# Token scores made by 32 rows in four column quarters and turned back, one weight product for all batches, and small operations moved to GpSimd

## The chip, the cores and the metric

One core of one Trainium2 chip runs the whole program. The metric is the time of one execution in device microseconds (us); the figure before is the median of three runs. A separate execution was recorded by the hardware profiler, and all rows below come from that one.

The engines are named as in the profile: PE (TensorE matmul), PEld (its weight load), DVE (VectorE), ACT (ScalarE), POOL (GpSimd) and SP (SyncE, whose queue issues every DMA here). Every engine works through its own instructions in the order of the program. An engine waits only where an operand or a buffer is not ready, and then everything behind that instruction on the same engine waits as well.

## The reference

The input is x (4 batches of 12,480 tokens of 128 numbers), 32 inducing vectors, two weight matrices and six coefficients. Twice an attention is taken, first of the 32 vectors over all tokens, then of all tokens over the 32 results; then a feed-forward with a rational activation follows.

```python
def mab(q, kv):
    s = scale * (q @ kv.transpose(0, 2, 1))
    s = s - s.max(-1, keepdims=True)
    a = np.exp(s)
    a /= a.sum(-1, keepdims=True) + 1e-09
    return a @ kv
h = mab(I, x)                 # I: the 32 vectors, for each of 4 batches
x = mab(x, h)                 # (4 * 12480, 128)
h = x @ w_in                  # to 2048 columns
P = a[0] + a[1] * h + a[2] * h * h + a[3] * h * h * h
Q = 1.0 + np.abs(b[0]) * np.abs(h) + np.abs(b[1]) * h * h
return (P / (Q + 1e-6)) @ w_out
```

## The kernel before

**Units and ticks.** A batch is cut into 26 blocks of 480 tokens, a block into 8 units (two slices of 128 of the 2048 columns each), so there are 4 x 26 x 8 = 832 units. `fast_ticks` walks through them, one unit to a tick. In tick t the PE makes the hidden values of unit t + 1 (`first`: two matmuls `hp`, two more `hp<-same,by` in every other unit), DVE masks a unit and does one `scalar_tensor_tensor` over it (`l<-u,all,hp`), ACT takes a logarithm or a sigmoid of a pair of units or an absolute value, and for the unit 15 ticks back DVE or POOL makes the last product. For the unit 17 ticks back the PE adds the two slices to the output of the block (`second`: `po<-l,w_out`, four instructions). After the eighth unit of a block two matmuls add a linear part (`po<-at,st`), for which `lin` of that batch must be there. Five logarithm ticks (`TURNS`) and five sigmoid ticks take turns, and ACT loads a table at every turn.

**Side work.** All that the units need is made in between by two generators. `ahead` makes what a batch needs: `pass1` (scores of the 32 vectors against the tokens, `pc`, then the exponential `e`), `pooled` (the pooled rows `HT`), `piece` (the stack `st` of `HT` times `w_in`, split into two halves by `split`), `linear` (the linear part `lin`) and `bounded` (a check of the range, which for batch 0 also takes maxima of the weights, `w_max`). `attend` runs `pass3`: for groups of 4 blocks it makes the scores of the tokens against the 32 pooled rows (`pd`), their maxima (`amx`), the differences (`a`), the exponential, the sums and quotients (`quotients`: `asm`, then the product on POOL), turns the result (`pa`), and splits it into two f16 halves `hl`, which `spread` sends by eight DMAs to a pair of blocks (`at`). A group of 4 blocks lasts for 32 units. A batch has seven groups, six of 4 blocks and one of 2, so there are 28; group 0 of batch 0 is made before the units begin.

**The order.** The order is written out ahead by `side`, once in a tick. Each `yield` names an engine and a planned cost. A tick gives 0.36 us to DVE ("v"), 0.9 to POOL ("g") and 0.75 to the PE ("pe"), saved up to a cap (1.45, 2.5 and 1.7 in one tick); in the first ticks, to tick 15, 2.9 of "v" and 2.0 of "pe" are given anew each time. A generator takes several steps of one kind in a tick and stops when the kind changes. A `yield "wait"` costs a tick, and work handed to ACT (`act`) costs two. Exponentials are put out only in the tick in which the logarithms end (t = 12, 22, 32, ...). One PSUM bank (`misc`) serves both generators, who hold it from the matmul to the last reader. `attend` has its turn first, but only once the linear part of batch 0 is there; the first two ticks are spent on the last two pieces of batch 0. Where a unit needs something that the plan has not reached (`at` of its pair of blocks, a piece of `st`, or `lin`), `until` writes all missing steps of both generators at that place, whatever they cost.

**Scores before.** In `pass3`, 16 matmuls of a group have 120 tokens as stationary operand and the 32 pooled rows as moving one, so that tokens lie on partitions. In f32 each matmul is two instructions. **Linear part before.** `linear` makes, for each batch, 16 products of `w_in` with `HT` (`pgt`), has ACT scale and shift them (`gt`), and `linear2` multiplies them by the 16 slices of `w_out` (`pl`), repeats the 32 rows four times with `ident4` (`prep`), and `thirds` splits them.

Of the kernel before, what the change touches and what calls it, by code (L numbers as in the profile page):

```python
# [21 lines left out]
M = 32  # L22
C = 128
HB = 4
BT = HB * TP
CEPS = 1.0 + 1e-6
LAM = 0.625
A16 = 2.0 ** 14
S16 = 2.0 ** 6
Z = A16 * S16  # L30
# [162 lines left out]
class Kernel:  # L193
# [79 lines left out]
    def setup(self):  # L273
        nc, cp = self.nc, self.cp
        self.ind = cp.tile([C, M], F32, name="ind")
        nc.sync.dma_start(out=self.ind, in_=self.ind_c)
        self.ident = cp.tile([P, P], F32, name="ident")
        make_identity(self.tc.nc, self.ident)
        self.ones = cp.tile([1, 4], F32, name="ones")
        nc.vector.memset(self.ones, 1.0)  # L280
        self.ident4 = cp.tile([M, 4, M], F32, name="ident4")
        for j in range(4):
            nc.vector.tensor_copy(out=self.ident4[:, j], in_=self.ident[0:M, 0:M])
# [155 lines left out]
    def pooled(self, b, own=None):  # L439

        nc, ap = self.nc, self.ap
# [21 lines left out]
        for g in range(self.NG):  # L463
            nb = min(4, self.NB - 4 * g)
# [5 lines left out]
            for k in range(HB * nb):  # L470
                j, c = divmod(k, HB)
# [26 lines left out]
        self.free()  # L498
        yield "pe", 0.3
        pt = self.misc(f"HT{b}")  # L500
        nc.tensor.matmul(pt[:, 0:4 * M], H, self.ident4.rearrange("p a m -> p (a m)"), start=True, stop=True)
        yield "v", 0.2
        while own is None and self.scored < b - 2:
            yield "wait", 0
# [40 lines left out]
        return t if self.fast else t.bitcast(F32)  # L545

    def split(self, b, which, st, g):
        cost = 0.34
# [10 lines left out]
        self.ready_cols[b].add(which)  # L559

    def linear(self, b):

        nc, ap = self.nc, self.ap
        for f in range(self.NF):
            yield "pe", 0.2
            if f == 0:
                pt = self.misc(f"pgt{b}").rearrange("p (f m) -> p f m", m=M)
            nc.tensor.matmul(pt[:, f], self.w_in[:, P * f:P * f + P], self.HT[b][:, 0:M], start=True, stop=True)
        gt = ap.tile([P, 512], F32, tag="gs", name=f"gt{b}", bufs=2)[:, 0:self.NF * M].rearrange("p (f m) -> p f m", m=M)
        yield from self.act(lambda: nc.scalar.activation(gt, pt[:, 0:self.NF], AF.Identity, bias=self.params.lin_shift, scale=self.params.lin_scale))  # L570
        self.free()
        self.gt[b] = gt

    def linear2(self, b):
        nc, ap = self.nc, self.ap
        gt = self.gt[b]
        for f in range(self.NF):
            yield "pe", 0.25
            if f == 0:
                pl = self.misc(f"pl{b}")  # L580
            nc.tensor.matmul(pl[0:M, 0:C], gt[:, f], self.w_out[:, f], start=(f == 0), stop=(f == self.NF - 1))
        yield "v", 0.2
        lin = ap.tile([M, C], F32, tag="H", name=f"lin{b}")
        nc.vector.tensor_copy(out=lin, in_=pl[0:M, 0:C])
        self.free()
        yield "pe", 0.3
        pr = self.misc(f"prep{b}")
        nc.tensor.matmul(pr[:, 0:C], self.ident4.rearrange("p a m -> p (a m)"), lin, start=True, stop=True)
        yield "v", 0.2
        g = ap.tile([P, 512], F32, tag="gs", name=f"gl{b}", bufs=2)  # L590
        nc.vector.tensor_scalar(out=g[:, 0:C], in0=pr[:, 0:C], scalar1=Z * Z / A16, scalar2=None, op0=ALU.mult)
        self.free()
        yield "v", 0.6
        self.thirds(b, g)
        self.ready_cols[b].add("linear")

    def thirds(self, b, g):

        V, lin = self.nc.vector, self.lin[b]
        top, rest = slice(0, 2 * M), slice(2 * M, 4 * M)  # L600
        parts = self.ap.tile([P, 3, C], BF16, tag="parts", name=f"parts{b}")
        hi, mid, low = (parts[:, i] for i in range(3))
# [41 lines left out]
    def pass3(self, b, groups):  # L644
# [4 lines left out]
        for fours in groups:  # L649
            wide = ap.tile([TP, 2, HB, 4, M], F32, tag="a", name=f"a{b}_{fours[0]}")  # L650
            todo = []
            for i, r in enumerate(fours):
                nb = min(4, self.NB - 4 * r)
                mx = ap.tile([TP, 4, HB, 1], F32, tag="amx", name=f"amx{b}_{r}")[:, 0:nb]
                yield from self.landed("b", b, r)
                for j in range(HB * nb):
                    yield "pe", 0.15
                    if j == 0:
                        pc = self.misc(f"pd{b}_{r}")
                    if j % HB == 0:  # L660
                        xT = self.cols[b, "b"].take()
                    nc.tensor.matmul(pc[0:TP, M * j:M * j + M], xT[:, TP * (j % HB):TP * (j % HB) + TP], self.HT[b][:, 0:M], start=True, stop=True)
                    if j % HB == HB - 1:
                        self.cols[b, "b"].read()
                a = wide[:, i, :, 0:nb]
                sc = pc[0:TP, 0:HB * nb * M].rearrange("p (j c m) -> p j c m", m=M, c=HB)
# [3 lines left out]
                nc.vector.tensor_tensor(out=a.rearrange("p c j m -> p j c m"), in0=sc, in1=mx.broadcast_to((TP, nb, HB, M)), op=ALU.subtract)  # L670
                self.free()
                todo.append((r, nb, a))
            done = []
# [18 lines left out]
    def quotients(self, b, r, nb, a):  # L692
        nc, ap = self.nc, self.ap
        rows = slice(0, M * nb)
        sm = ap.tile([TP, HB, 4, 1], F32, tag="asm", name=f"asm{b}_{r}")[:, :, 0:nb]
        yield "v", 0.7
# [5 lines left out]
        (nc.vector if self.boot else nc.gpsimd).tensor_tensor(out=a, in0=a, in1=sm.broadcast_to(a.shape), op=ALU.mult)  # L702
# [32 lines left out]
    def ahead(self):  # L735

        if self.fast:
            yield from self.linear(0)
            yield from self.linear2(0)
            yield from self.bounded(0)  # L740
        for b in range(1, self.B):
            self.cols[b, "a"] = self.columns(b, "a")
            yield "wait", 0
            yield "wait", 0
            yield from self.pass1(b)
            yield from self.pooled(b)
            while self.left < b - 2:
                yield "wait", 0
            self.stacks(b)
            for j in range(self.F // 512):  # L750
                yield from self.piece(b, j)
            if self.fast:
                yield from self.linear(b)
                yield from self.linear2(b)
                yield from self.bounded(b)

    def groups(self, first):
# [262 lines left out]
    def main(self, fast):  # L1020
        nc, p = self.nc, self.params
        self.fast = fast
        self.HT, self.st, self.gt, self.at, self.full = {0: self.HT[0]}, {}, {}, {}, None
# [90 lines left out]
```

## Time and profile before

| | us |
|---|---|
| median of 3 runs | 2411.62 |
| lowest and highest | 2408.2, 2415.34 |
| the profiled execution | 2418.05 |
| span of its rows | 2416.2 |
| PE busy | 2222.9 |
| ACT busy | 2181.9 |
| DVE busy | 2152.9 |
| POOL busy | 1454.6 |

The span runs from the first to the last instruction. The shares lie close together, so that an average over the span does not tell which engine sets the pace; the stretches have to be read one by one. Matmuls are pipelined, so the time of one instruction is longer than the distance between two of them.

### The profile page before, as it was taken

The numbers are of one execution on the slowest core, as the hardware profiler recorded it, in microseconds if no ns is written. First come the engines' busy times: TensorE is split into PE (matmuls) and PEld (weight loads), VectorE is DVE, ScalarE is ACT, GpSimd is POOL, SyncE is SP. The second block draws the span as 40 slices with busy tenths as digits, with TensorE's granted clock in tenths as the row PEclk, the third lists the DMA queues.
The fourth block names the chain that finished last, engine by engine and source line by source line (L and its number), as shares of the span: only waits on it lengthen the run. The fifth ranks groups of instructions, "written<-read, shape, count | busy, mean of one in ns | idle before, by whom it ended". The sixth has DMA issues, their size and how long they took to land.

```text
span 2416.2 us, 25742 instructions
## 1 busy us (share of the span) xinstructions
PE 2222.9 (92%) x8462; PEld 1077.6 (45%) x8462; DVE 2152.9 (89%) x2386; ACT 2181.9 (90%) x1550; POOL 1454.6 (60%) x997
## 2 busy tenths in 40 slices
PE   4279989899999999899999999999999999999997
PEld 2144544344554444344544444445444444444443
DVE  1679999889999999899989998899899999999995
ACT  1059999999989999999989999999899999999996
POOL 0316566666656666566656675666566666666666
PEclk6559999999999999999999999999999999999999
DMA  9312210022112220032022210221101100000000
GB/s 235 88 33 82 82 46 22 16 70 74 33 49 66 67 81 17 21 82 62 29 66 73 83 33 29 62 63 48 34 29 39 32 21 25 21 17 21 17 17 18
DMA packets 117112, 121.02 MB, mean 50 GB/s; under 512 B 13289, under 2 KB 115561, under 8 KB 116969
## 3 DMA queue, kind: packets, MB, share of 16 engines
q1 hardware_dynamic: 116969, 119.28, 17.8%
q8 instruction: 69, 1.13, 0.2%
q14 instruction: 74, 0.61, 0.1%
HBM read 80.89 MB, written 25.56 MB: 44 GB/s over the span
## 4 chain that ended last, share of the span: by engine, by line
PE 50%; DVE 20%; ACT 16%; issue 9%; POOL 3%; DMA 2%; SPq 1%; DVEq 0%; POOLq 0%; ACTq 0%
PE po L177 31%; ACT u L177 13%; PE hp L177 11%; DVE l L177 11%; DVE u L177 4%; PE pd L177 3%; ACT L177 2%; DVE asm L177 1%; POOL l L177 1%; PE ph L177 1%; DMA xw<-x_t 1%; SPq L177 1%; DMA xTw<-x_c 1%; POOL u L177 1%; PE pgt L177 1%
## 5 line engine op out<-in xcount | busy, mean ns | idle before, releaser
L177 PE MATMUL po<-l,w_out 128*128 128x480 f32 x3328 | 1566.0, 575 | 5.4 <-DVE oT L177 3.1
L177 DVE SCALAR_TENSOR_TENSOR l<-u,all,hp 128x960 f32<-128x960 f32 x832 | 1001.9, 1204 | 74.7 <-ACT u L177 58.2
L177 POOL TENSOR_TENSOR l<-u 128x960 f32<-128x960 f32 x416 | 930.9, 2238 | 34.7
L177 POOL TENSOR_SCALAR u<-l,all 128x960 f32<-128x960 f32 x416 | 446.6, 1073 | 800.4 <-DVE l L177 690.9
L177 PEld LDWEIGHTS po<-l,w_out 128*128 128x128 f32 x3328 | 617.2, 191 | 383.0 <-issue 220.4
L177 ACT ACTIVATE u<-u,all 128x1920 f32<-128x1920 f32 x416 | 770.1, 1888 | 1.0
L177 ACT ACTIVATE u<-u 128x1920 f32<-128x1920 f32 x416 | 732.5, 1795 | 5.2 <-DVE l L177 4.0
L177 PE MATMUL hp<-at,st 128*128 128x480 f16 x1664 | 478.3, 369 | 58.8 <-DVE l L177 54.0
L177 DVE SCALAR_TENSOR_TENSOR l<-l,all,u 128x960 f32<-128x960 f32 x416 | 529.3, 1273 | 2.0 <-ACT u L177 2.0
L177 DVE TENSOR_SCALAR u<-hp 128x960 int32<-128x960 int32 x416 | 476.8, 1146 | 43.4 <-PE hp L177 42.0
L177 ACT ACTIVATE u<-hp,all 128x960 f32<-128x960 f32 x416 | 436.1, 1048 | 86.9 <-PE hp L177 82.8
L177 PEld LDWEIGHTS <-st 128*128 128x128 f16 x1872 | 182.2, 98 | 539.8 <-issue 523.4
L177 PE MATMUL hp<-same,by 96*128 96x480 f16 x832 | 239.9, 369 | 41.7 <-DVE u L177 35.3
L177 ACT ACT_TABLE_LOAD x194 | 248.9, 1283 | 4.0 <-PEq L1107 0.7
L177 PEld LDWEIGHTS <-by 96*128 96x128 f16 x832 | 82.0, 99 | 231.8 <-issue 204.4
L177 DVE COPY oT<-po 128x480 f32<-128x480 f32 x104 | 67.9, 653 | 64.0 <-PE po L177 63.8
L177 PEld LDWEIGHTS pd<-HT,xTb 128*120 128x120 f32 x832 | 101.3, 195 | 16.9 <-issue 11.7
L177 PE MATMUL pd<-HT,xTb 128*120 128x32 f32 x832 | 98.1, 274 | 2.2 <-DMA xTb<-x_c 1.5
L177 PE MATMUL po<-at,st 128*128 128x480 f16 x208 | 59.1, 366 | 0.0
L177 ACT ACTIVATE a<-a 120x512 f32<-120x512 f32 (+2 forms) x21 | 14.9, 728 | 43.5 <-DVE a L177 43.3
L177 PE MATMUL pa<-ident,a 120*128 120x120 f32 (+1 forms) x112 | 17.7, 284 | 36.5 <-DVE a L177 25.0
L177 POOL TENSOR_TENSOR cv<-cv 128x384 f32<-128x384 f32 (+2 forms) x11 | 12.0, 1087 | 59.2 <-DVE cv L177 55.9
(110 smaller groups left out, 609.9 us busy)
## 6 DMA issues: line engine op xcount, KB each, us to landing
xTb<-x_c SPq DMA_DIRECT2D x104, 240.0 KB, 2.8
out<-oT SPq DMA_DIRECT2D x104, 240.0 KB, 2.0
xTa<-x_c SPq DMA_DIRECT2D x78, 240.0 KB, 3.4
x<-x_t SPq DMA_DIRECT2D x78, 240.0 KB, 4.4
at<-hl SPq DMA_DIRECT2D x416, 30.0 KB, 1.8
xw<-x_t SPq DMA_DIRECT2D x8, 720.0 KB, 14.6
xTw<-x_c SPq DMA_DIRECT2D x5, 960.0 KB, 11.9
raw<-w_in SPq DMA_DIRECT2D x4, 480.0 KB, 12.1
```

Of the source, the lines that this page charges most:

```text
L177: ins = call(*args, **kw)
```

## The change

- `pass3` has the 32 pooled rows as stationary operand: four matmuls of a group, one for each block of 480 tokens, write four quarters of 32 partitions of one PSUM bank. DVE copies this 128 x 480 tile to SBUF (`sT`), the bank is given free, and the PE turns it back in four transposes of 120 tokens each (`ps`), from which maxima and differences are taken as before, with the two middle dimensions of the tile exchanged.
- `products`, run once at the start, multiplies `w_in` (scaled) by `w_out` to one 128 x 128 matrix `w_two`, in four rounds of four transposes, an ACT pass, four matmuls and a DVE add, and makes `base` from the shift and the sum over `w_out`. `linear` is then, for each batch, one matmul of `HT` with `w_two` and one DVE operation; `linear2` and `ident4` are gone.
- In `split` the f16 copy of a piece runs on POOL in place of DVE. In `quotients` the small addition to the sums runs on POOL, and six plain waits of a tick each stand around it, the reciprocal and the product.

```diff
 linear(b)
-        for f in range(self.NF):
-            yield "pe", 0.2
...
-            nc.tensor.matmul(pt[:, f], self.w_in[:, P * f:P * f + P], self.HT[b][:, 0:M], start=True, stop=True)
...
-        for f in range(self.NF):
-            yield "pe", 0.25
...
-            nc.tensor.matmul(pl[0:M, 0:C], gt[:, f], self.w_out[:, f], start=(f == 0), stop=(f == self.NF - 1))
...
+        yield "pe", 0.25
         pr = self.misc(f"prep{b}")
-        nc.tensor.matmul(pr[:, 0:C], self.ident4.rearrange("p a m -> p (a m)"), lin, start=True, stop=True)
+        nc.tensor.matmul(pr[:, 0:C], self.HT[b], self.w_two, start=True, stop=True)
+        yield "v", 0.25
...
+        nc.vector.scalar_tensor_tensor(out=g[:, 0:C], in0=pr[:, 0:C], scalar=Z * Z / A16, in1=self.base, op0=ALU.mult, op1=ALU.add)
 products()
+        nc.gpsimd.tensor_scalar(out=level, in0=self.ident, scalar1=0.0, scalar2=p.lin_shift, op0=ALU.mult, op1=ALU.add)
+        for i in range(2):
+            yield "v", 1.2
+            c = slice(C // 2 * i, C // 2 * (i + 1))
+            nc.vector.tensor_reduce(out=w_sum[:, c], in_=self.w_out[:, :, c].rearrange("p f d -> p d f"), axis=mybir.AxisListType.X, op=ALU.add)
+        yield "pe", 0.25
...
+        yield "v", 0.25
...
+        for j in range(self.NF // 4):
+            for i in range(4):
+                yield "pe", 0.22
...
+                nc.tensor.transpose(out=pt[:, P * i:P * i + P], in_=self.w_in[:, P * (4 * j + i):P * (4 * j + i) + P], identity=self.ident)
...
+            yield from self.act(lambda: nc.scalar.activation(wt, pt, AF.Identity, bias=0.0, scale=p.lin_scale))
+            self.free()
+            for i in range(4):
+                yield "pe", 0.25
...
+                nc.tensor.matmul(pl[:, 0:C], wt[:, P * i:P * i + P], self.w_out[:, 4 * j + i], start=(i == 0), stop=(i == 3))
+            yield "v", 0.25
...
 pass3(b, groups)
-                for j in range(HB * nb):
-                    yield "pe", 0.15
...
-                    nc.tensor.matmul(pc[0:TP, M * j:M * j + M], xT[:, TP * (j % HB):TP * (j % HB) + TP], self.HT[b][:, 0:M], start=True, stop=True)
...
+                yield "pe", 1.0
+                pd = self.misc(f"pd{b}_{r}")
+                for j in range(nb):
+                    nc.tensor.matmul(pd[M * j:M * j + M, 0:BT], self.HT[b][:, 0:M], self.cols[b, "b"].take(), start=True, stop=True)
+                    self.cols[b, "b"].read()
+                yield "v", 0.6
+                sT = ap.tile([P, BT], F32, tag="sT", name=f"sT{b}_{r}")
+                nc.vector.tensor_copy(out=sT[rows], in_=pd[rows, 0:BT])
+                self.free()
+                for c in range(HB):
                     yield "pe", 0.15
...
+                    nc.tensor.transpose(out=ps[0:TP, c, rows], in_=sT[rows, TP * c:TP * c + TP], identity=self.ident[rows, rows])
 split(b, which, st, g)
-        yield 0, cost, 0
+        yield 0, 0, 0.7
...
-            self.cast(self.nc.vector, st, g)
+            self.cast(self.nc.gpsimd, st, g)
 quotients(b, r, nb, a)
         nc.vector.tensor_reduce(out=sm[:, :, :, 0], in_=a, axis=mybir.AxisListType.X, op=ALU.add)
+        yield "wait", 0
+        engine.tensor_scalar(out=sm, in0=sm, scalar1=1.0, scalar2=1e-9, op0=ALU.mult, op1=ALU.add)
+        yield "wait", 0
+        yield "wait", 0
         yield "v", 0.25
-        nc.vector.tensor_scalar(out=sm, in0=sm, scalar1=1e-9, scalar2=None, op0=ALU.add)
         nc.vector.reciprocal(out=sm, in_=sm)
+        yield "wait", 0
         yield "g", 1.2
...
+        yield "wait", 0
+        yield "wait", 0
```

## Rows read from the trace of the kernel before

**Rows 1.** Busy time of each engine in some stretches of the span, by the view of windows. The columns are the stretch, its length, the busy time and number of instructions of PE, PEld, DVE, ACT and POOL, the granted clock of the PE, the share of the DMA engines and GB/s.

```profile
123.00:147.00 24.00, 21.34 (x88) 14.08 (x89) 14.30 (x15) 8.90 (x10) 2.31 (x2) 0.63 0.00 0
147.00:178.00 31.00, 17.10 (x64) 10.52 (x63) 25.83 (x37) 24.19 (x17) 3.28 (x2) 0.56 0.22 64
...
242.00:423.00 181.00, 169.89 (x630) 82.86 (x629) 168.98 (x185) 169.42 (x120) 111.34 (x73) 1.00 0.17 50
604.00:966.00 362.00, 348.80 (x1305) 172.50 (x1304) 338.68 (x371) 338.97 (x239) 229.74 (x146) 1.00 0.17 52
1148.00:1389.00 241.00, 232.96 (x907) 116.58 (x907) 223.15 (x250) 220.25 (x154) 147.42 (x92) 0.99 0.21 63
1631.00:1812.00 181.00, 173.06 (x647) 88.25 (x646) 168.90 (x180) 164.49 (x116) 113.89 (x70) 0.98 0.12 37
2114.00:2356.00 242.00, 231.61 (x708) 103.22 (x707) 226.94 (x207) 241.41 (x167) 161.28 (x98) 1.00 0.05 18
```

**Rows 2.** Who waited for whom over the whole span, from the view of waits: total us, times, longest.

```profile
ACT u L177 <- PE hp L177: 82.8, 52, 9.6
...
PEld pa L177 <- POOL a L177: 14.5, 7, 3.1
...
PE pa L177 <- POOL a L177: 11.5, 6, 2.6
```

**Rows 3.** The PE in order of time, at one group of token scores. The columns are start, length (to the modelled end of the last one), what it is and how many in a row.

```profile
211.11 2.40 PE L177 MATMUL pd<-HT,xTb 128*120 128x32 f32 x22
213.34 1.05 PE L177 MATMUL po<-l,w_out 128*128 128x480 f32 x2
```

**Rows 4.** The PE in order of time, in two other places and in the same columns: the four score matmuls of a group in the first pass, and the four transposes of a group, each with the main matmul behind it.

```profile
190.30 1.01 PE L177 MATMUL pc<-xTa,ind 128*32 128x480 f32 x8
191.24 1.07 PE L177 MATMUL po<-l,w_out 128*128 128x480 f32 x2
...
200.20 0.57 PE L177 MATMUL pa<-ident,a 120*128 120x120 f32 x4
200.61 2.59 PE L177 MATMUL po<-l,w_out 128*128 128x480 f32 x6
```

**Rows 5.** Groups of instructions of one shape over the whole span: what, how often, total busy us and mean ns of one, then the idle time of the engine before them.

```profile
L177 DVE COPY oT<-po 128x480 f32<-128x480 f32 x104 | 67.9, 653 | 64.0 <-PE po L177 63.8
...
L177 DVE TENSOR_SCALAR asm<-asm 120x16 f32<-120x16 f32 x24 | 18.2, 759 | 0.6
...
L177 DVE TENSOR_SCALAR st<-gs 128x512 f16<-128x512 f32 x14 | 6.8, 486 | 9.7 <-ACT gs L177 9.7
...
L177 DVE TENSOR_REDUCE w_max<-w_in 128x1 f32<-128x512 f32 x8 | 5.0, 678 | 0.0
...
L177 ACT ACTIVATE gt<-pgt,all 128x512 f32<-128x512 f32 x4 | 3.1, 772 | 0.0
```

**Rows 6.** The instructions that write or read the sums `asm`, smallest, median and largest length in ns, over the whole span.

```profile
L177 DVE TENSOR_SCALAR asm<-asm x28: 156/174/1841, 105.3 to 2111.2; 120x16 f32<-120x16 f32 x24, 120x8 f32<-120x8 f32 x4
...
L177 POOL TENSOR_TENSOR a<-a,asm x27: 619/1050/1975, 197.8 to 2116.2; 120x512 f32<-120x512 f32 x23, 120x256 f32<-120x256 f32 x4
```

**Rows 7.** The linear part of batch 0 on the PE, in order of time.

```profile
127.54 4.31 PE L177 MATMUL pgt<-HT,w_in 128*128 128x32 f32 x20
...
132.45 2.61 PE L177 MATMUL pgt<-HT,w_in 128*128 128x32 f32 x12
...
144.32 1.93 PE L177 MATMUL pl<-w_out,gt 128*32 128x128 f32 x16
```

**Rows 8.** ACT in order of time in the first units; in brackets the idle time before the instruction and what ended it.

```profile
135.89 1.06 ACT L177 ACTIVATE u<-hp,all 128x960 f32<-128x960 f32 x1 [9.58 <-PE hp L177]
...
146.80 1.06 ACT L177 ACTIVATE u<-hp,all 128x960 f32<-128x960 f32 x1 [3.40 <-PE hp L177]
...
167.95 1.06 ACT L177 ACTIVATE u<-hp,all 128x960 f32<-128x960 f32 x1 [6.34 <-PE hp L177]
```

**Rows 9.** The first group of token scores, made before the units, all engines in order of time: maxima, exponential, transposes, the second halves, and the first matmul of the units.

```profile
102.45 0.69 DVE L177 TENSOR_REDUCE amx<-pd 120x16 f32<-120x512 f32 x1 [0.44 <-DVE w_out L177]
...
103.90 0.63 ACT L177 ACTIVATE a<-a 120x512 f32<-120x512 f32 x1 [42.67 <-DVE a L177]
...
106.62 1.03 PE L177 MATMUL pa<-ident,a 120*128 120x120 f32 x4 [24.98 <-DVE a L177]
...
108.29 0.66 DVE L177 SCALAR_TENSOR_TENSOR hl<-pa,hl 128x480 f16<-128x480 f32 x1 [1.82 <-ACT hl L177]
...
112.35 0.98 PE L177 MATMUL hp<-at,st 128*128 128x480 f16 x4 [1.71 <-POOL st L177]
```

**Rows 10.** ACT in order of time around one exponential of token scores.

```profile
190.01 1.28 ACT L177 ACT_TABLE_LOAD   x1
191.30 0.63 ACT L177 ACTIVATE a<-a 120x512 f32<-120x512 f32 x1
191.95 1.28 ACT L177 ACT_TABLE_LOAD   x1
```

**Rows 11.** SP's queue in order of time, one pair of blocks sent: start, length of the eight issues together.

```profile
707.03 4.95 SPq L177 DMA_DIRECT2D at<-hl  x8
```

**Rows 12.** The same transfer in the view of the DMAs: how often, KB of one, median us from issue to landing.

```profile
at<-hl SPq DMA_DIRECT2D x416, 30.0 KB, 1.8
```

More of the change, by code (lines that the diff above doesn't have):

```diff
@@ L500, in pooled @@
         pt = self.misc(f"HT{b}")
-        nc.tensor.matmul(pt[:, 0:4 * M], H, self.ident4.rearrange("p a m -> p (a m)"), start=True, stop=True)
+        nc.tensor.matmul(pt[:, 0:4 * M], H, self.ident[0:M, 0:M].rearrange("p (a m) -> p a m", a=1).broadcast_to((M, 4, M)), start=True, stop=True)
         yield "v", 0.2
@@ L559, in split, with products @@
         self.ready_cols[b].add(which)
+    def products(self):
+        nc, cp, ap, p = self.nc, self.cp, self.ap, self.params
+        self.w_two = cp.tile([C, C], F32, name="w_two")
+        self.base = cp.tile([P, C], F32, name="base")
+        both = ap.tile([P, 512], F32, tag="gs", name="both", bufs=2)
+        level, w_sum = both[:, 0:P], both[:, P:P + C]
+        nc.gpsimd.tensor_scalar(out=level, in0=self.ident, scalar1=0.0, scalar2=p.lin_shift, op0=ALU.mult, op1=ALU.add)
[4 more added lines that the diff above has]
+        yield "pe", 0.25
+        pb = self.misc("base")
+        nc.tensor.matmul(pb[:, 0:C], level, w_sum, start=True, stop=True)
+        yield "v", 0.25
+        nc.vector.tensor_scalar(out=self.base, in0=pb[:, 0:C], scalar1=Z * Z / A16, scalar2=None, op0=ALU.mult)
+        self.free()
+        for j in range(self.NF // 4):
+            for i in range(4):
+                yield "pe", 0.22
+                if i == 0:
+                    pt = self.misc(f"pgt{j}")
+                nc.tensor.transpose(out=pt[:, P * i:P * i + P], in_=self.w_in[:, P * (4 * j + i):P * (4 * j + i) + P], identity=self.ident)
+            wt = ap.tile([P, 512], F32, tag="gs", name=f"wt{j}", bufs=2)
+            yield from self.act(lambda: nc.scalar.activation(wt, pt, AF.Identity, bias=0.0, scale=p.lin_scale))
+            self.free()
+            for i in range(4):
+                yield "pe", 0.25
+                if i == 0:
+                    pl = self.misc(f"pl{j}")
+                nc.tensor.matmul(pl[:, 0:C], wt[:, P * i:P * i + P], self.w_out[:, 4 * j + i], start=(i == 0), stop=(i == 3))
+            yield "v", 0.25
+            if j == 0:
+                nc.vector.tensor_copy(out=self.w_two, in_=pl[:, 0:C])
+            else:
+                nc.vector.tensor_tensor(out=self.w_two, in0=pl[:, 0:C], in1=self.w_two, op=ALU.add)
+            self.free()
@@ L600, in thirds @@
         top, rest = slice(0, 2 * M), slice(2 * M, 4 * M)
-        parts = self.ap.tile([P, 3, C], BF16, tag="parts", name=f"parts{b}")
-        hi, mid, low = (parts[:, i] for i in range(3))
+        parts = g[:, 3 * C:4 * C].bitcast(BF16).rearrange("p (i d) -> p i d", d=C)
+        hi, mid = parts[:, 0], parts[:, 1]
         x, y, z = (g[:, C * i:C * i + C] for i in range(3))
@@ L653, in pass3 @@
                 nb = min(4, self.NB - 4 * r)
-                mx = ap.tile([TP, 4, HB, 1], F32, tag="amx", name=f"amx{b}_{r}")[:, 0:nb]
+                rows = slice(0, M * nb)
+                mx = ap.tile([TP, HB, 4, 1], F32, tag="amx", name=f"amx{b}_{r}")[:, :, 0:nb]
                 yield from self.landed("b", b, r)
-                for j in range(HB * nb):
-                    yield "pe", 0.15
[L658 to L661, printed above, removed]
-                    nc.tensor.matmul(pc[0:TP, M * j:M * j + M], xT[:, TP * (j % HB):TP * (j % HB) + TP], self.HT[b][:, 0:M], start=True, stop=True)
-                    if j % HB == HB - 1:
-                        self.cols[b, "b"].read()
+                yield "pe", 1.0
[6 more added lines that the diff above has]
+                nc.vector.tensor_copy(out=sT[rows], in_=pd[rows, 0:BT])
+                self.free()
+                for c in range(HB):
+                    yield "pe", 0.15
+                    if c == 0:
+                        ps = self.misc(f"ps{b}_{r}").rearrange("p (c n) -> p c n", c=HB)
+                    nc.tensor.transpose(out=ps[0:TP, c, rows], in_=sT[rows, TP * c:TP * c + TP], identity=self.ident[rows, rows])
                 a = wide[:, i, :, 0:nb]
-                sc = pc[0:TP, 0:HB * nb * M].rearrange("p (j c m) -> p j c m", m=M, c=HB)
+                sc = ps[0:TP, :, rows].rearrange("p c (j m) -> p c j m", m=M)
                 yield "v", 0.7
@@ L737, in ahead @@
         if self.fast:
+            yield from self.products()
             yield from self.linear(0)
-            yield from self.linear2(0)
             yield from self.bounded(0)
@@ L753, in ahead @@
                 yield from self.linear(b)
-                yield from self.linear2(b)
                 yield from self.bounded(b)
@@ L1022, in main @@
         self.fast = fast
-        self.HT, self.st, self.gt, self.at, self.full = {0: self.HT[0]}, {}, {}, {}, None
+        self.HT, self.st, self.at, self.full = {0: self.HT[0]}, {}, {}, None
         self.ready_cols = {b: set() for b in range(self.B)}
```

27 lines of the change are left out of this document (3 added, 24 removed).

## The prediction, made before the changed kernel was run

> **What bounds the kernel now.** I read the share of busy time first and set it aside, because PE, ACT and DVE lie within a few per cent of each other. Then I read the windows, to find which engine fills each stretch. Where no side work runs, ACT is the bound: it is busy for 241.41 of 242 us, with PE and DVE below it [rows 1]. Where `pd`, `pooled` or the linear part of a later batch is made, no engine is full: in the four stretches of 242 to 423, 604 to 966, 1148 to 1389 and 1631 to 1812 us ACT idles 11.6, 23.0, 20.8 and 16.5 us [rows 1]. The view of waits names what ACT idles for: 82.8 us in 52 places before the absolute value of a unit, which wants `hp` from the PE [rows 2]. The PE comes late there because the side matmuls stand in its queue in front of `hp`. So a microsecond taken from the PE is worth something in these stretches only, and never more than until DVE or ACT is full there: 181 - 169.42, 362 - 338.97, 241 - 223.15 and 181 - 168.90 us [rows 1] give 11.6 + 23.0 + 17.9 + 12.1 = 64.6 us as the ceiling. A third place is the start, where ACT idles 9.58, 3.40 and 6.34 us behind `pgt`, `pl` and the first `pd` [rows 7, 8].
>
> **Part 1, the scores.** Today 22 of the 32 instructions of a group hold the PE from 211.11 to 213.34 us [rows 3], 101 ns each, so a group costs 3.24 us. The new form is that of the first pass, 32 columns of weights, 480 moving ones and four quarters of partitions, and there eight instructions hold the PE from 190.30 to 191.24 us, 0.94 us; four transposes hold it for 0.41 us [rows 4]. A group then costs 1.35 us, 1.89 less. Some 20 of the 28 groups are made in the four stretches (five of batch 0, seven of batch 1, five of batch 2, three of batch 3), 37.8 us. The others stand where ACT is full, and bring nothing.
>
> DVE gets one copy of 128 x 480 from PSUM for each group, 0.653 us by the copy of the output [rows 5]. It loses the small addition to the sums, 0.759 us on average [rows 5], and the f16 copies of fourteen pieces, 0.486 each [rows 5]. So 28 x 0.653 = 18.3 us come and 18.2 + 6.8 = 25.0 go: DVE's load is about what it was. The addition is short by itself: its median is 0.174 us and its longest 1.841, while POOL's products beside it last to 1.975 us [rows 6], so most of its mean is waiting. The Trainium skill explains it: SBUF - State Buffer, section "SBUF: two separate sides", says that VectorE and GpSimd share a pair of ports as an exclusive lock, held for the whole instruction. By that rule the wait leaves DVE with the instruction, and the trace's spread agrees.
>
> POOL has room (161.28 of 242 us [rows 1]) for 28 small additions, between 0.17 us by DVE's median [rows 6] and 1 us with a wait, and for 14 copies of 128 x 512, between DVE's 0.49 [rows 5] and twice that; I take the lower ends, hidden. What is queued behind them on POOL is the last product of a unit, two ticks ahead of its use, so that they cost nothing until POOL is 5 us late. The six waits in `quotients` make a group six ticks later but give POOL time: the PE's 11.5 us and its weight loads' 14.5 us before `pa` [rows 2] should mostly go.
>
> **Part 2, the linear part.** Each of batches 1 to 3 loses 64 instructions on the PE (about 0.1 us each at the full clock, by the `pd` row [rows 3]), 6.5 us less one small matmul, so 19 us in all, and 0.772 us of ACT [rows 5]. Its splitting on DVE stays.
>
> **Sum of the stretches.** Parts 1 and 2 take 37.8 + 19 = 57 us from the PE under a ceiling of 64.6. All of it would be the upper end. The lower end is 15 us: DVE is busy 899.7 of 965 us there [rows 1] and holds `hp` up by itself too. I take 36, the middle, since DVE's load stays and the PE's long bursts were the larger part of the wait.
>
> **Before the units.** The copy and the four transposes enter the chain of the first group in front of the maxima, which start at 102.45 us with DVE just free [rows 9]: 0.65 + 1.03 (transposes at the lower clock) plus two handovers of some 0.2, about +2 us. `pg` of the first pieces stands behind it on the PE, so nothing hides it. The ends are 0 and +4.
>
> **The first units.** Here I counted the plan tick by tick with the rules of `side`. Before, `lin` of batch 0 is planned at t = 10. Now t = 0 and 1 go to pieces, t = 2 to 4 to the reductions and `base`, and each of the four rounds takes five ticks (transposes, two for ACT, matmuls, DVE): matmuls at 8, 13, 18, 23, the last addition not before 24. But unit 7 needs `lin` in `second` at t = 24. So `until` writes the last additions, `linear`, and the whole scoring of group 1 there; `attend` may only start then, its exponential would come at t = 32, and unit 32 wants `at` at t = 31: a second `until`. My count finds no third: group 2 is sent at t = 60 (wanted at 63), the first group of batch 1 at 201 (wanted at 207), and `HT` of batch 1 comes at 166 (172 before).
> What goes: the bursts of `pgt`, `pl` and `pd` [rows 7], behind which ACT idled 19.3 us [rows 8]; I take 16. What comes: two reductions of 1024, twice 1.36 us by 0.678 for 512 [rows 5], 3 us; the first forced place, about 6 us of DVE and PE in series, of which ACT, whose sigmoids are of units already made, shows 0 to 6, say 2; the second forced place. There an exponential with one extra table load of 1.28 [rows 10], then 5.05 us from exponential to second halves as in the first group (103.90 to 108.95 [rows 9]), then eight issues of 4.95 in all [rows 11] and 1.8 to land [rows 12]: 13 us, in which ACT has about 5 us of its own work, so 8, between 4 and 14 (`ahead` is written out there too, with the first four loads of pass 1 of batch 1 on SP ahead of the eight issues, which SP reaches long before). And w_max, 5 us of DVE, moves to fuller ticks: 1 us. Together -16 + 3 + 2 + 8 + 1 = -2.
>
> **Sum.** -36 + 2 - 2 = -36 us. The profiled execution of 2418.05 us (span 2416.2) becomes 2382; it lies 6.4 above the median of 2411.62, from which I take the same 36: **2376 us**.
>
> **The rivals.**
> (a) DVE becomes the bound. For it: it is 93% busy in the stretches, and each group's scores now pass it once more, in PSUM reads that cannot overlap. Then only the lower end of 15 remains, less 2 us at the boot and a second forced place of 10 or more: 2405 to 2411. Against it: its own sum is even. A sentence of the Trainium skill speaks for it: TensorEngine Tiling (Array Packing), section "PSUM Bottleneck", says that tiling quickens the TensorE but not the emptying of PSUM, which may become the bottleneck. By that rule the time is that of this rival; the waits shown so far name `hp`, not a copy.
> (b) Slower: the plan falls behind. If the six waits put off the first group of a batch past its first unit, `until` writes the chain there, about 13 us of exposed chain (as above). It decides from 6 ticks more than I counted in batch 1. With three such places and the two at the start at their upper ends, 3 x 13 + 12 + 6 - 36 = +21: 2433. Against it: the plan before, counted in the same way, has no forced place, and its ticks hold 20 and 12 instructions of `pgt` and 16 of `pl`, as the trace has them [rows 7].
> (c) More: PE's lateness was all of ACT's idle time there; the stretches give 57 and the start 10: 2343.
> (d) It does not do what it says: the quarters run one behind the other, eight times 0.4 us (six of 480 columns take 2.59 with the tail [rows 4]), and a group costs what it did, with copy and transposes on top. Then only the linear part's half pays: about 2405. The first pass speaks against it [rows 4].
>
> **How the numbers follow.** Forecast (2350 to 2404) 0.64, (a) 0.13, (b) 0.09, (c) 0.11, (d) 0.03. A measurement of this kernel can tell about 0.3%, 7 us, from no change, so faster means under 2404.4. Faster: forecast, (c), and a third of (a) and (d), 0.80; same: most of the rest of (a) and (d), 0.10; slower: (b) and a tail, 0.10. The range leaves out (b) and the far half of (c) and (d's) tail: 2348 to 2412, which takes in the bounds of 15 and 57 us with the ends of the boot and the forced places.
>
> **What would show it.** `pd` in eight instructions of about 0.95 us a group, with ACT's wait for `hp` down from 82.8 to about 40 us; two clusters of forced work near units 24 and 31, the second with ACT idle some 8 us; first `hp` about 2 us later; the mean of `asm` gone from DVE. Wrong would be: ACT idle as long as before with DVE full (a), more forced places at the first units of batches (b), or quarters that run in turn (d).

## The result, and the profile after

The changed kernel took 2359.54 us (median; 2357.84 to 2361.61) against 2412.11 of the kernel before, measured beside it: ratio 0.9784 (95% interval 0.9769 to 0.9798), or -52.6 us. The forecast was 2376, -36 us, with a range of 2348 to 2412. The sign and the range held; the gain was half as large again as the sum said, so a term of the sum is mis-sized.

The profiled execution after has a span of 2359.4 us. First its windows, in stretches that hold about the same units as the five late stretches of [rows 1] (two to four units more in three of them), in the same columns:

```profile
240.00:413.00 173.00, 164.06 (x555) 73.47 (x554) 165.52 (x182) 171.87 (x121) 111.52 (x76) 0.97 0.20 62
587.00:943.00 356.00, 338.54 (x1194) 152.06 (x1193) 345.41 (x368) 346.14 (x245) 235.74 (x162) 0.99 0.19 57
1121.00:1353.00 232.00, 223.87 (x754) 99.48 (x753) 222.77 (x239) 231.17 (x164) 151.63 (x100) 0.99 0.19 59
1592.00:1757.00 165.00, 159.75 (x517) 71.54 (x516) 159.11 (x154) 164.56 (x116) 109.45 (x69) 1.00 0.14 43
2057.00:2299.00 242.00, 231.83 (x709) 103.52 (x708) 226.47 (x208) 241.41 (x167) 161.85 (x99) 1.00 0.05 18
```

The last stretch, where ACT was full already, is as long as before. In the first four ACT now idles 1.1, 9.9, 0.8 and 0.4 us, where it idled 11.6, 23.0, 20.8 and 16.5. From 240 us on the bound is ACT nearly everywhere. Then the waits over the whole span (us, times, longest), to be held against [rows 2]:

```profile
DVE l L177 <- ACT u L177: 76.6, 80, 3.3
...
ACT u L177 <- PE hp L177: 36.9, 17, 7.2
```

ACT's wait for `hp` fell from 82.8 us in 52 places to 36.9 in 17, and DVE now waits for ACT longest of these. PE's and PEld's waits before `pa` for POOL's product (11.5 and 14.5 us) have no row any more; one wait of 1.2 us for another instruction of POOL is left there. One group of scores on the PE, as in [rows 3] (start, length, what):

```profile
308.28 1.01 PE L177 MATMUL pd<-xTb,HT 128*32 128x480 f32 x8
309.22 1.07 PE L177 MATMUL po<-l,w_out 128*128 128x480 f32 x2
...
313.76 0.60 PE L177 MATMUL ps<-ident,sT 128*120 128x128 f32 x4
314.20 0.97 PE L177 MATMUL po<-l,w_out 128*128 128x480 f32 x2
```

The eight instructions hold the PE for 0.94 us and the four transposes for 0.44: 1.38 us a group, by 1.35 forecast. The first units, ACT in order of time:

```profile
192.65 1.06 ACT L177 ACTIVATE u<-hp,all 128x960 f32<-128x960 f32 x1 [7.19 <-PE hp L177]
...
204.17 0.63 ACT L177 ACTIVATE a<-a 120x512 f32<-120x512 f32 x1
209.73 0.57 ACT L177 ACTIVATE hl<-pa 128x480 f16<-128x480 f32 x1 [4.93 <-PE pa L177]
...
218.88 1.06 ACT L177 ACTIVATE u<-hp,all 128x960 f32<-128x960 f32 x1 [1.31 <-PE hp L177]
```

These are the two forced places, near units 24 and 31: ACT idles 7.19 us at the first, and 4.93 and 1.31 at the second. And the start, all engines, as in [rows 9]:

```profile
100.45 0.66 DVE L177 COPY sT<-pd 128x480 f32<-128x480 f32 x1 [0.44 <-DVE w_out L177]
...
101.17 1.11 PE L177 MATMUL ps<-ident,sT 128*120 128x128 f32 x4 [24.03 <-DVE sT L177]
102.31 0.69 DVE L177 TENSOR_REDUCE amx<-ps 120x16 f32<-120x512 f32 x1 [1.20 <-PE ps L177]
```

From the copy to the maxima it is 1.86 us: the forecast's +2. Net it can't be read: DVE was free for the copy 2.0 us earlier than it was for the maxima before, the first `hp` stands at 112.15 us by 112.35, and the start itself varies by more (the table at the end of the experiments).

### The profile page after: what moved, and what is told of

The parts are those of the page before. It is cut to its first block, busy times and chain, and to the rows that moved or that the text cites. A ratio compares the mean times of both kernels' runs of the same rounds, so it can differ in the third digit from the quotient of the medians.

```text
span 2359.4 us, 24314 instructions
## 1 busy us (share of the span) xinstructions
PE 2163.3 (92%) x7744; PEld 978.0 (41%) x7744; DVE 2152.3 (91%) x2372; ACT 2177.5 (92%) x1551; POOL 1476.2 (63%) x1039
## 4 chain that ended last, share of the span: by engine, by line
PE 33%; ACT 27%; DVE 21%; issue 12%; POOL 2%; DMA 2%; SPq 2%; DVEq 0%; ACTq 0%; POOLq 0%
ACT u L177 22%; PE po L177 22%; DVE l L177 11%; PE hp L177 8%; DVE u L177 5%; ACT L177 3%; SPq L177 2%; POOL l L177 1%; DMA xTw<-x_c 1%; PE ph L177 1%; DVE cv L177 1%; PE pc L177 1%; DVE gl L177 1%; DVE oT L177 1%; POOL u L177 1%
## 5 line engine op out<-in xcount | busy, mean ns | idle before, releaser
L177 POOL TENSOR_TENSOR l<-u 128x960 f32<-128x960 f32 x416 | 929.8, 2235 | 34.6
L177 ACT ACTIVATE u<-hp,all 128x960 f32<-128x960 f32 x416 | 435.4, 1047 | 37.5 <-PE hp L177 36.9
L177 POOL TENSOR_TENSOR cv<-cv 128x384 f32<-128x384 f32 (+2 forms) x11 | 11.9, 1086 | 57.0 <-DVE cv L177 53.7
L177 ACT ACTIVATE e<-e,nmc 128x960 f32<-128x960 f32 (+1 forms) x16 | 15.6, 993 | 31.7 <-DVE nmc L177 31.5
L177 DVE TENSOR_SCALAR_CACHE_REDUCE e<-pc 128x240 f32<-128x240 f32 (+1 forms) x56 | 20.8, 400 | 24.6 <-PE pc L177 24.6
L177 PE MATMUL ps<-ident,sT 128*120 128x128 f32 (+1 forms) x112 | 16.8, 273 | 24.4 <-DVE sT L177 24.0
```

Source lines behind the costliest of these rows:

```text
L177: ins = call(*args, **kw)
```

## The experiments

The first four runs were made on two theories. Theory P is the prediction's: the PE's long side bursts held up `hp`, so the shorter scores and linear part carry the gain. Theory S is its rival: the small operations and the waits in `quotients`, to which the sum gave no gain, carry the larger part. Their before was 2412.72 us.

**The new scores alone**, in the kernel before:

```diff
+                    nc.tensor.matmul(pd[M * j:M * j + M, 0:BT], self.HT[b][:, 0:M], self.cols[b, "b"].take(), start=True, stop=True)
+                nc.vector.tensor_copy(out=sT[rows], in_=pd[rows, 0:BT])
+                    nc.tensor.transpose(out=ps[0:TP, c, rows], in_=sT[rows, TP * c:TP * c + TP], identity=self.ident[rows, rows])
```

> The kernel before with the new scores alone (four column quarters, copy, four transposes); linear part, f16 copies and quotients as before. Theory P (the PE's long side bursts held hp back, and the time saved is PE time): the scores carry the larger part of the 53 us, -25 to -35 us, near 2382 us. Theory S (the moves to GpSimd carry the larger part, by DVE's waits for GpSimd and the PE's wait for POOL's product): -5 to -15 us, near 2402. By the count of the plan one place is forced, at the first unit of batch 1.

2402.52 us, ratio 0.996 (0.9945 to 0.9975): -10. The waits show a part of why so little of 37.8 us of PE came through:

```profile
ACT u L177 <- PE hp L177: 62.6, 57, 8.8
...
PEld pa L177 <- POOL a L177: 20.2, 11, 3.1
```

ACT waits 20 us less for `hp`, but the weight loads stand 20.2 us before `pa` where they stood 14.5. A larger part is the forced place that the expectation had counted. It is there, at unit 206 (ACT and PE in order of time):

```profile
688.90 0.57 ACT L177 ACTIVATE hl<-pa 128x480 f16<-128x480 f32 x1 [7.04 <-PE pa L177]
...
693.25 0.96 PE L177 MATMUL hp<-at,st 128*128 128x480 f16 x2 [4.38 <-DMA at<-hl]
...
698.30 1.06 ACT L177 ACTIVATE u<-hp,all 128x960 f32<-128x960 f32 x1 [3.07 <-PE hp L177]
...
704.23 1.06 ACT L177 ACTIVATE u<-hp,all 128x960 f32<-128x960 f32 x1 [1.48 <-PE hp L177]
```

The unit waits for the transfer of `at` that was written out just ahead of it, and ACT idles 11.6 us in three pieces.

**The new linear part alone** (`products` and `linear` of the change, scores and `quotients` of before):

```diff
+        nc.tensor.matmul(pr[:, 0:C], self.HT[b], self.w_two, start=True, stop=True)
```

> The kernel before with the new linear part alone (one product of the weights, one matmul for each batch). Theory P: three batches lose 6.5 us of PE each, but the plan forces lin of batch 0 at unit 24 and a place at the first unit of batch 1; -5 to -15 us, near 2402. Theory S: about the same, -5 us, since no move to GpSimd is in it.

2406.83 us, ratio 0.9975 (0.9965 to 0.9984): -6. Here too the counted place at unit 206 is there, and ACT idles 10.6 us at it:

```profile
688.00 0.57 ACT L177 ACTIVATE hl<-pa 128x480 f16<-128x480 f32 x1 [4.70 <-PE pa L177]
...
696.49 1.06 ACT L177 ACTIVATE u<-hp,all 128x960 f32<-128x960 f32 x1 [2.16 <-PE hp L177]
...
704.62 1.06 ACT L177 ACTIVATE u<-hp,all 128x960 f32<-128x960 f32 x1 [3.69 <-PE hp L177]
```

**The small operations and the six waits alone** (`split` and `quotients` of the change in the kernel before):

```diff
-            self.cast(self.nc.vector, st, g)
+            self.cast(self.nc.gpsimd, st, g)
+        yield "wait", 0
+        engine.tensor_scalar(out=sm, in0=sm, scalar1=1.0, scalar2=1e-9, op0=ALU.mult, op1=ALU.add)
+        yield "wait", 0
```

> The kernel before with the moves to GpSimd alone (f16 copies of the pieces, the small addition to the sums, the six waits). Theory P: DVE loses its waits of 18 us in places where it is seldom the last, -3 to -10 us, near 2406. Theory S: -25 us or more, 2387 or less.

2378.13 us, ratio 0.9855 (0.9831 to 0.9879): -34.6. This is the largest of the three, and theory S's.

**The score matmuls made three times**, in the changed kernel, with the plan as it is, so that a group costs the PE again what it cost before (redundant work; the last pass stays):

```diff
+                for again in range(1 if self.boot else 3):
+                    for j in range(nb):
+                        nc.tensor.matmul(pd[M * j:M * j + M, 0:BT], self.HT[b][:, 0:M], xTs[j], start=True, stop=True)
```

> The changed kernel, in which the four score matmuls of every group in the units are made three times over, so that a group holds the PE for 3 x 0.94 + 0.41 = 3.2 us as before the change, with all planned costs, and so the order of everything else, unchanged. The repeats write the same values again. Theory P: the gain of the scores is lost, +25 to +40 us on the changed kernel, 2385 to 2400 us. Theory S: +0 to +10 us, 2360 to 2370.

2377.53 us, ratio 0.9849 (0.9827 to 0.987): +18 on the changed kernel, between the theories. That is more than the scores alone gave in the kernel before, where the forced place took back a part.

The next four (before: 2415.48 us) took the small edits apart.

**The six waits alone**, in the kernel before; addition and copies stay on DVE:

```diff
+        yield "wait", 0
         nc.vector.tensor_scalar(out=sm, in0=sm, scalar1=1e-9, scalar2=None, op0=ALU.add)
+        yield "wait", 0
+        yield "wait", 0
```

> The kernel before with the six plain waits of a tick in the quotients alone; the small addition stays on DVE, the f16 copies too. Three theories on which of the small edits gives the 34.6 us that the run of the small operations alone gained. Theory W (order: the PE no longer stands in front of pa until POOL's product is there, 26 us of waits of PE and PEld in [rows 2]): -20 to -30 us here, PE's wait before pa near 0, ACT's wait for hp near 60 us. Theory L (DVE's lock: the addition stood on DVE for 0.759 us on average by 0.174 median): -3 to -8 here, with the addition's mean as long as before. Theory C (the f16 copies): about 0.

2395.17 us, ratio 0.9914 (0.9891 to 0.9937): -20. Of PE's and PEld's waits before `pa` for POOL's product 0.2 us are left, and so far theory W holds. But DVE's long additions, which theory L expected to stay, went as well, so this run doesn't tell the two causes apart. The instructions that write `asm` (shortest, median and longest in ns), to be held against [rows 6]:

```profile
L177 DVE TENSOR_SCALAR asm<-asm x28: 154/167/519, 103.9 to 2085.2; 120x16 f32<-120x16 f32 x24, 120x8 f32<-120x8 f32 x4
```

The addition is still on DVE, and its longest is 0.519 us where it was 1.841. Its 24 full-size instances took 4.8 us (198 ns each) instead of 18.2.

**The addition on POOL alone**, without waits:

```diff
-        nc.vector.tensor_scalar(out=sm, in0=sm, scalar1=1e-9, scalar2=None, op0=ALU.add)
+        engine.tensor_scalar(out=sm, in0=sm, scalar1=1.0, scalar2=1e-9, op0=ALU.mult, op1=ALU.add)
```

> The kernel before with the small addition on POOL alone, no waits added, f16 copies on DVE. Theory W: PE waits in front of pa as long as before or longer, since POOL has one instruction more in that chain; -5 to +5 us. Theory L: -14 us or more (18.2 us of the addition leave DVE, of which 14 were waiting). Theory C: about 0.

2419.46 us, ratio 1.0021 (1.001 to 1.0032): +4. One instance, all engines:

```profile
302.47 0.67 DVE L177 TENSOR_REDUCE asm<-a 120x16 f32<-120x512 f32 x1
...
302.75 2.22 POOL L177 TENSOR_TENSOR l<-u 128x960 f32<-128x960 f32 x1
305.06 0.20 POOL L177 TENSOR_SCALAR asm<-asm 120x16 f32<-120x16 f32 x1
305.29 0.25 DVE L177 RECIPROCAL asm<-asm 120x16 f32<-120x16 f32 x1 [2.15 <-POOL asm L177]
```

On POOL the addition queues behind the last product of a unit (2.22 us), and DVE's reciprocal stands for it. Over the span:

```profile
DVE asm L177 <- POOL asm L177: 22.9, 15, 2.8
...
PEld pa L177 <- POOL a L177: 13.8, 8, 3.0
```

What DVE saved in busy time (2152.9 to 2133.3 us) it lost in waiting, and the wait before `pa` stayed. Theory L falls.

**The f16 copies on POOL alone:**

```diff
-            self.cast(self.nc.vector, st, g)
+            self.cast(self.nc.gpsimd, st, g)
```

> The kernel before with the f16 copies of the pieces on POOL alone. Theory W and theory L: -3 to +3 us (6.8 us leave DVE, POOL has the room). Theory C: -10 us or more.

2412.48 us, ratio 0.9981 (0.9969 to 0.9993): -3 by the medians, -5 by the ratio; not the 10 or more of theory C.

**The copies back on DVE, in the changed kernel:**

```diff
-            self.cast(self.nc.gpsimd, st, g)
+            self.cast(self.nc.vector, st, g)
```

> The changed kernel with the f16 copies of the pieces back on DVE. If they are worth little by themselves (theory W, theory L): -5 to +5 us on the changed kernel; below 0 if POOL's longer splits, beside which DVE's subtractions of the linear part took 2.2 us each, cost more than 6.8 us on DVE. If they carry a part of their own (theory C): +8 us or more.

2362.06 us, ratio 0.9785 (0.9769 to 0.9802): no different from the changed kernel. Theory C falls.

The last four (before: 2412.94 us).

**The waits and the addition, without the copies**, in the kernel before:

```diff
+        yield "wait", 0
+        engine.tensor_scalar(out=sm, in0=sm, scalar1=1.0, scalar2=1e-9, op0=ALU.mult, op1=ALU.add)
+        yield "wait", 0
+        yield "wait", 0
```

> The kernel before with all of the new quotients (six waits and the small addition on POOL), f16 copies left on DVE. The waits alone gave 20.8 us (call 2395, before 2415.5), the addition alone lost 4.0, the f16 copies alone gave 3.0. If these add up: -17 us. If the addition on POOL is worth something only once the waits give POOL its time (in the waits' run DVE had 4.8 us of the addition left): -25 to -32 us, and the f16 copies are the rest of the 34.6.

2396.3 us, ratio 0.9932 (0.9911 to 0.9953): -16.6. With the waits there, it makes no measurable difference on which engine the addition runs (0.9914 with it on DVE). But the three small edits do not add up: with the copies they gave 34.6 us, 18 more than here, while the copies alone gave 3.

**The changed kernel without the six waits:**

```diff
-        yield "wait", 0
         engine.tensor_scalar(out=sm, in0=sm, scalar1=1.0, scalar2=1e-9, op0=ALU.mult, op1=ALU.add)
-        yield "wait", 0
-        yield "wait", 0
```

> The changed kernel without the six waits (the addition stays on POOL). If the order of the quotients carries the gain in the changed kernel too: +18 to +30 us on the changed kernel, with PE's and PEld's waits before pa back at 20 us or more and the reciprocal on DVE waiting some 20 us for POOL. If new scores and linear part have taken over that gain (a shorter PE has room to stand still): +0 to +8 us. The plan has one forced place more here by the count (unit 207).

2384.94 us, ratio 0.9888 (0.9863 to 0.9912): +25 on the changed kernel. Both waits are back:

```profile
DVE asm L177 <- POOL asm L177: 19.4, 12, 2.2
PEld pa L177 <- POOL a L177: 18.6, 8, 4.3
```

And there is a forced place at unit 206, as in the two runs above, ACT in order of time:

```profile
689.39 0.57 ACT L177 ACTIVATE hl<-pa 128x480 f16<-128x480 f32 x1 [6.77 <-PE pa L177]
...
698.89 1.06 ACT L177 ACTIVATE u<-hp,all 128x960 f32<-128x960 f32 x1 [3.16 <-PE hp L177]
...
705.27 1.06 ACT L177 ACTIVATE u<-hp,all 128x960 f32<-128x960 f32 x1 [1.94 <-PE hp L177]
```

That place shows 11.9 us of the ACT idle time by itself, so the waits go with two things here: order among POOL, DVE and PE, and a plan that reaches unit 206 in time.

**The splitting of the linear part set apart**, in the changed kernel. After the change ACT still idles longest, 5.7 and 6.8 us, at the linear parts of batches 1 and 3, where DVE's subtractions took 2.3 us beside POOL:

```diff
+        for _ in range(3 if b else 0):
+            yield "wait", 0
         yield "v", 0.6
-        self.thirds(b, g)
+        yield from self.thirds(b, g)
```

> The changed kernel with three waits of a tick ahead of the splitting of the linear part of batches 1 to 3 and one between its three steps, so that DVE's subtractions no longer stand beside POOL's splits of the pieces. If DVE's 2.2 us subtractions there cause the 17 us that ACT idles at the three linear parts: -8 to -15 us on the changed kernel. If that idle time comes from PE's own side work at these places: -3 to +3.

2361.98 us, ratio 0.9784 (0.976 to 0.9808): nothing gained. That lies in the second range of the expectation (-3 to +3), and the first, -8 to -15, missed; that PE's own side work is the cause, as the second has it, isn't shown. The instructions that work on `gl`, in the changed kernel and then in this one:

```profile
L177 DVE TENSOR_SCALAR gl<-gl x8: 218/736/1144, 183.1 to 1553.1; 128x128 bf16<-128x128 f32 x8
L177 DVE TENSOR_TENSOR gl<-gl x8: 291/452/2344, 183.4 to 1554.2; 128x128 f32<-128x128 f32 x8
```

```profile
L177 DVE TENSOR_SCALAR st<-gl x12: 154/218/2252, 186.8 to 1663.0; 64x128 bf16<-64x128 f32 x12
L177 DVE TENSOR_SCALAR gl<-gl x8: 163/216/279, 185.7 to 1657.9; 128x128 bf16<-128x128 f32 x8
L177 DVE TENSOR_TENSOR gl<-gl x8: 291/293/2346, 186.0 to 1658.1; 128x128 f32<-128x128 f32 x8
```

The rounding to bf16 got short, but a subtraction still took 2.3 us, and the next step 2.25, beside the 2.2 us products of the units on POOL. ACT's two longest idle times after unit 32, 5.7 and 6.8 us, did go (none is over 2.7 us), and yet the late part is as long: that idle time came back elsewhere.

**The first units mended as well.** The transposes of the weights move ahead of the units, the product accumulates in one bank, and the second group of batch 0 gets no waits:

```diff
+        if fast:
+            self.turned_weights()
...
+            nc.tensor.matmul(pl[:, 0:C], self.wt[f // 8][:, P * (f % 8):P * (f % 8) + P], self.w_out[:, f], start=(f == 0), stop=(f == self.NF - 1))
...
+        first = b == 0 and r == 1
+        for _ in range(0 if first else 2):
+            yield "wait", 0
```

> The last kernel, and in addition the sixteen transposes of the weights and ACT's scaling of them are made before the first group of scores, the sixteen matmuls of the product accumulate in one bank, and the second group of batch 0 has no waits in its quotients. By the count no place is forced any more (linear part of batch 0 planned at tick 9). If the two forced places near units 24 and 31 cost what ACT idles there (7.2 and 7.5 us): -10 to -15 us against the kernel with the splitting apart, from which about 3 go for the transposes at the start: -7 to -12. If ACT makes up for the idle time later: 0 to +4. Together with the splitting apart about -20 us on the changed kernel, 2340.

2351.04 us (2350.68 to 2355.61), ratio 0.9749 (0.9724 to 0.9774): the fastest of all, 8 us below the changed kernel by the ratios and 10.9 below the run with the splitting apart, where 7 to 12 were expected. The 2340 expected in all were not reached, since the splitting gave nothing. ACT at the places that were forced:

```profile
178.43 0.63 ACT L177 ACTIVATE a<-a 120x512 f32<-120x512 f32 x1
...
191.83 1.06 ACT L177 ACTIVATE u<-hp,all 128x960 f32<-128x960 f32 x1 [0.53 <-PE hp L177]
192.79 0.56 ACT L177 ACTIVATE hl<-pa 128x480 f16<-128x480 f32 x1
```

The exponential comes 26 us earlier, and nothing idles for it.

**Where the time went in each profiled execution.** The span of each, cut at the starts of DVE's `l<-u,all,hp` of units 0 and 32 (us; one execution each):

| kernel | to unit 0 | 0 to 32 | 32 to the end |
|---|---|---|---|
| before | 123.1 | 100.1 | 2193.0 |
| scores alone | 122.8 | 91.0 | 2190.0 |
| linear alone | 120.2 | 96.6 | 2185.0 |
| small operations and waits | 119.1 | 96.4 | 2161.6 |
| waits alone | 121.9 | 100.7 | 2169.0 |
| addition alone | 120.1 | 98.3 | 2199.0 |
| copies alone | 118.7 | 93.9 | 2201.3 |
| waits and addition | 122.4 | 103.3 | 2168.3 |
| **after** | 120.0 | 101.7 | 2137.7 |
| after, copies on DVE | 122.2 | 101.8 | 2135.2 |
| after, scores three times | 117.1 | 104.6 | 2153.5 |
| after, no waits | 117.2 | 101.6 | 2161.4 |
| after, splitting apart | 121.8 | 103.1 | 2139.5 |
| the last kernel | 117.7 | 92.5 | 2138.4 |

The first column scatters by 5 us among kernels with the same start (after and its variants without the waits, with copies on DVE, with the splitting apart), so nothing is read from it.

## Why the prediction was right, and where its sum was not

**What bounds the kernel: right.** ACT's wait for `hp` was the time to be had. It fell to 36.9 us, by "about 40" forecast; DVE came closer but is not the bound (rival a), and the quarters run side by side (rival d).

**Late stretches, -36: the term was mis-sized.** From unit 32 on, 55.3 us went. What failed is the third paragraph of part 1. It saw that the waits give POOL time and that PE's 11.5 and the weight loads' 14.5 us before `pa` "should mostly go", and then gave that no price. The runs price it: the waits alone take 24.0 us from the late part (2193.0 to 2169.0). What is left, 55.3 - 24.0 = 31.3 us, stands for everything else, where the sum had 36. So the sum for PE time was near, and a second gain beside it was left out. Without the waits the changed kernel loses nearly the same, 23.7 (2137.7 to 2161.4), but that is in part luck: 11.9 us of it can be the forced place at unit 206, which the kernel before has not, so that some 12 are left for the order itself (an estimate).

The 11.5 and 14.5 us are also one standing seen in two rows, as in this instance of the kernel before:

```profile
1305.31 0.41 PEld L177 LDWEIGHTS pa<-ident,a 120*128 120x128 f32 x4 [1.68 <-POOL a L177]
1305.31 0.63 PE L177 MATMUL pa<-ident,a 120*128 120x120 f32 x4 [1.22 <-POOL a L177]
```

So it was 14.5 us that could go there, not 26, and the 24.0 need more than that wait.

**Scores and linear part.** Trebling the score matmuls costs 15.8 us in the late part, about 0.4 of the 37.8 us of PE time; in the sum it was 36 of 57, about 0.6. Alone in the kernel before, scores and linear part took only 3.0 and 8.0 us from the late part, together less than half of the 31.3. The forced place at unit 206, which neither the kernel before nor the changed one has, accounts for most of the difference: units 192 to 208 took 56.1 and 54.1 us in these two runs, 46.5 in the kernel before and 41.3 in the changed one. Put back by that time (9.6 and 7.6 us) or by ACT's idle time there (11.6 and 10.6), an estimate, the two are worth 28 to 33 us, near the 31.3, and the scores 12.6 to 14.6, near the 15.8 of trebling them. The two together without the small edits were not run. Why the plan is in time at unit 206 with the waits and late without them wasn't followed.

**The small addition: wrong in its mechanism.** "The wait leaves DVE with the instruction" is not what happened: alone, the wait turned into DVE standing 22.9 us for POOL. What removes it are the ticks around the addition, on either engine. Right behind the sum, the addition meets the product that POOL has just begun, and ends with it (kernel before):

```profile
305.96 0.67 DVE L177 TENSOR_REDUCE asm<-a 120x16 f32<-120x512 f32 x1
...
306.24 2.22 POOL L177 TENSOR_TENSOR l<-u 128x960 f32<-128x960 f32 x1
...
306.67 1.83 DVE L177 TENSOR_SCALAR asm<-asm 120x16 f32<-120x16 f32 x1
```

That is the last product of a unit; the product of [rows 6], which the prediction set beside the addition, comes only after it. The Trainium skill's rule in SBUF - State Buffer, section "SBUF: two separate sides", that where a VectorE operation uses the ports shared with GpSimd (in a two-port mode, or with two SBUF inputs), whichever engine begins first holds them for the whole instruction, fits this: an addition of 0.17 us took up to 1.84, and a subtraction of 0.29 up to 2.34, beside POOL products of 2.2. The rule tells that one of the two waits; it doesn't say that moving the instruction to the other engine ends the wait, and here it didn't.

**POOL's copies at nothing: right in the changed kernel** (2362.06 with them on DVE). In the kernel before they are worth 6 to 7 us in units 0 to 32 (100.1 to 93.9, and 103.3 to 96.4), and in the late part they change the time by +8.3 without the waits and by -6.7 with them, with no sign of their own. Why the order reacts so is open.

**The start, +2:** 1.86 us in the chain. The sign named for it, a first `hp` 2 us later, was not seen, because DVE was free earlier.

**The first units, -2: +1.6 measured.** There are two forced places, as counted, and none at the first units of batches 1 to 3 (rival b). The second was priced at 8 us: ACT idles 4.93 + 1.31, and loads one table more (1.28), 7.5. The first was priced at 2 and showed 7.19. The PE in order of time at that place, with the idle time before an instruction in brackets:

```profile
184.68 0.99 PE L177 MATMUL po<-at,st 128*128 128x480 f16 x2 [2.93 <-DVE st L177]
...
188.15 3.99 PE L177 MATMUL po<-l,w_out 128*128 128x480 f32 x6
...
191.98 0.57 PE L177 MATMUL hp<-at,st 128*128 128x480 f16 x2
```

and the windows just before it and at it, in the columns of [rows 1]:

```profile
160.00:180.00 20.00, 19.37 (x78) 9.62 (x76) 14.31 (x15) 19.94 (x16) 11.86 (x7) 0.99 0.00 1
180.00:184.00 4.00, 1.14 (x6) 0.71 (x6) 2.54 (x8) 4.00 (x4) 0.00 (x0) 1.00 0.76 245
184.00:192.00 8.00, 6.55 (x13) 2.42 (x14) 7.87 (x13) 1.45 (x1) 2.11 (x2) 0.57 0.40 123
```

From 180 to 184 us the PE was busy for 1.14 us only, it stood 2.93 us for DVE's last step, and then ran its backlog at a granted clock of 0.57, that is mostly at the lower level of 1.2 GHz, where the 20 us from 160 on had 0.99. Six main matmuls took 3.99 us there by 2.59 [rows 4], and `hp` was queued behind them. The step priced the series that is written out, and not the slower PE behind it. The last kernel, which has neither place, needs 9.2 us less for these units; that they were a loss inside the gain is shown by it.

**The rivals' sums.** One slips: by 57 + 10 us off the median, rival (c) stands at 2345 us, not 2343. Nothing hangs on it.

**What stays open:** how the 24 us of the waits divide between PE, no longer standing before `pa` (14.5 us at most), and DVE, whose busy time fell by 22.5 us (2152.9 to 2130.4). Both went together in every run that had the waits.

## What to carry to other kernels

When a profile shows an engine waiting for a short chain across three engines, price the wait itself before the work around it: a plain delay in the written order, so that each link is ready when its engine comes to it, was worth 20 us here. An instruction that is slow because it lands beside another engine's long one was cured here by another place in the order, not by the other engine's queue. And in a plan with due times, count the due times for every run, also those with one edit: work done once at the start pushed other work past its due time, which took back 9 us here, and one such place made the scores alone look worth a quarter of what they are.

## What was not expected of the hardware

Of 0.174 us by its median, the same DVE instruction took 1.84 us right behind the sum, and at most 0.52 us when placed a tick later, with the six idle ticks as the only change to the kernel. And a forced series cost more than its length, since the PE came back from it at a granted clock of 0.57: six main matmuls took 3.99 us by 2.59.
